# Two more row groups of batch 1 in seven block products, an earlier weight sum and other planned lengths of attention

## The chip, the core and the metric

The kernel runs on one core of one Trainium2 chip. The metric is the device time of one execution in microseconds (us). A core has TensorE (PE; its weight loads are listed apart as PEld), VectorE (DVE), ScalarE (ACT), GpSimd (POOL) and SyncE (SP), which here only issues transfers. Each engine works through its own list of instructions in order; semaphores hold an instruction until what it needs is there.

## What is computed

Chunked attention with a few memory keys, then a Fourier mix, a normalisation and two matrices with a Relu between them:

```python
# attention: 4 batches, 8 heads, 768 rows, 64 per head; chunks of 32 rows,
# each sees 16 rows to its left, 8 to its right and 8 memory rows
scores = scale * np.matmul(q_c, k_full.transpose(0, 1, 3, 2))
a = softmax(scores)
out[:, :, c_start:c_end] = np.matmul(a, v_full)
...
# x: 4 x 768 x 512, the heads side by side
mixed = np.real(np.fft.fft(np.fft.fft(x, axis=1), axis=2))
u = x + mixed
un = (u - mean(u)) / np.sqrt(var(u) + 1e-06)
ch = np.maximum(un @ w_ch1, 0.0) @ w_ch2      # w_ch1: 512 x 2048, w_ch2: 2048 x 512
return u + ch
```

## The kernel before

**Tiles.** A batch's 768 rows are six tiles of 128. Attention takes a pair of heads at a time, n = 0 to 15, four pairs a batch: loads of q and k from POOL's queue and of v from SP's, turns of q and k (on TensorE for batches 0 to 2, as transfers from SP's queue for batch 3), two groups of scores (`e_scores`, line 461), exponentials on ACT, values (`e_values`, line 485) and a division on DVE. `fourier(b)` then folds the rows on DVE (`zy`, `pq`, `ff`, `hi`, `lo`), multiplies by tables of cosines and sines on TensorE (`e_rows` at line 557, `e_columns` at line 727) and adds the result to the rows. For batches 1 to 3 the mirrored rows take a way through memory: out by `e_rows_out` (POOL, line 591), turned by `e_rows_turn` (SP, line 595), back by `e_mirror` (POOL, line 600), added by `e_sum_back` (DVE, line 615).

**Normalisation.** `e_stats` leaves mean and variance of a tile (line 741). A batch is then treated in one of two ways. In the plain way `e_un` writes mean - u (line 748), the Relu takes it with scale -1, and 1 / sqrt(var), made for the whole batch by `e_rstd` on POOL (line 785), multiplies the sum at the very end in `e_res` (line 828). In the other way `e_scale` on POOL (line 764) makes 1 / sqrt(var) and the shift for two tiles at a time, and `e_un` writes the normalised rows (line 752). `e_flip` turns a tile by a transfer from SP's queue (line 776) into `unT`, which has five buffers. The tiles `rs` of `e_scale` and `rstd` of `e_rstd` share two buffers.

**The two matrices.** A batch has three groups (b, j) of 256 rows: tiles 0 and 3, 4 and 5, 1 and 2 (`SLOT`). The first matrix, `e_ch1` (line 803), is eight steps of eight matmuls with 256 columns, each followed by a Relu into `hT` (line 812), of which there is one buffer. The second matrix of a plain group, `e_ch2` (line 821), is 2 x 16 matmuls with 512 columns, and `e_res` adds each half to u. A group in the list `FAST` does it as seven block products. There hT of the group is a 2 x 2 of blocks (two halves of the 2048 inner values, two tiles of rows) and w_ch2 a 2 x 2 of blocks (the same two halves, two halves of 256 columns). `e_s` (line 858) makes sums and differences of the blocks of hT on DVE, `e_w2t` (line 845) four of the weights, once for the whole kernel. `e_prod` (line 870) is eight matmuls with 256 columns for each of seven products, in the order 1, 2, 5, 6, 3, 7, 4, into the banks x, v and w; `e_add` (line 875) adds a product, or a running sum of them, to a half of u. The first three weight sums go to a tile of their own, which takes the place of hT of (0, 1); the fourth overwrites one block of w_ch2, so it waits for the last plain group. Products wait for the first three sums, product 4 for the fourth as well.

**The order.** Nothing is left to chance at run time: `Plan` simulates the engines with a length for each task and writes out the instructions in the order in which its tasks start. Attention and the Fourier mix have ranks in the order in which they are added; the two matrices have ranks from `MLPS` on, so they fill what the others leave of TensorE; Relus, residuals, sums on hT and adds have the lowest ranks and go first on their engines. The weight sums have ranks from `MLPS` on. After 45 us a task on TensorE that is no filler may be placed up to `SLACK` = 0.7 us before its inputs are due. `shortest(24, 1.5)` draws 24 disturbances of the ranks of all tasks after batch 0's attention and Fourier mix and keeps the order whose planned end is first. PSUM banks (`acc` and `mlp`, two each) are taken and given back in the plan; ph, the products' banks and one of the two value tiles take whichever of the two kinds came free first. The buffers of rs, rstd and the statistics are not in the plan.

`attention(n)`, lines 971 to 1045, adds the tasks of a pair with their lengths; `columns_of(b, t_rest)` those from the columns to the turned tiles; `layer1`, `layer2` and `weight_sums` those of the two matrices.

Of the kernel before, what the change touches and what calls it, by code (L numbers as in the profile page):

```python
# [205 lines left out]
def kernel(  # L206
# [12 lines left out]
    B, H, S, D = q.shape  # L219
# [44 lines left out]
    qs = [spool.tile([P, 2, RB * D], BF16, name=f"qs{i}") for i in range(NS)]  # L264
# [6 lines left out]
    kTb = [spool.tile([P, NT, P], BF16, name=f"kTb{i}") for i in range(NKT)]  # L271

    TURNED = 3
    FAST = [(b, j) for b in range(2, B) for j in range(3)]
    EVEN = {b for b, j in FAST}
    cp_q = "p h j d -> p h (j d)"
    HP = H // 2
    seq = [(b, pr) for b in range(B) for pr in (0, 2, 1, 3)]
# [138 lines left out]
    def e_turn_q(n):  # L417
        tr_of[n] = trq = aps.tile([P, S], BF16, tag="tr", bufs=1, name="trq")
        turn(trq, qs[n % NS][0:QP], ident_b[0:QP, 0:QP])
# [317 lines left out]
    def e_stats(b, kt):  # L737
# [3 lines left out]
        nc.vector.bn_stats(st6, xs[b][:, kt, :])  # L741
        nc.vector.bn_aggr(mu_of[b][:, kt, :], st6)

    def e_un(b, kt):
        un_of[b, kt] = un = fpool.tile([P, DM], FP16, tag="un", bufs=6, name="un")

        if b not in EVEN:
            nc.scalar.activation(un, xs[b][:, kt, :], AFT.Identity, bias=mu_of[b][:, kt, 0:1],
                                 scale=-1.0)
            return  # L750
        rs = rs_of[b][:, kt]
        nc.scalar.activation(un, xs[b][:, kt, :], AFT.Identity, bias=rs[:, 1:2], scale=rs[:, 0:1])  # L752
# [22 lines left out]
    def e_flip(b, kt):  # L775
        nc.sync.dma_start_transpose(unT(b, kt), un_of.pop((b, kt)))
# [29 lines left out]
    def e_relu(b, j, i):  # L806
        if i == 0:
            shape = [P, 2, HH, 2 * P]
            hT_of[b, j] = (wpool.tile(shape, FP16, tag="w2t", bufs=1, name="hT") if (b, j) == (0, 1) else
                           fpool.tile(shape, FP16, tag="hT", bufs=1, name="hT"))  # L810
        ph = ph_of.pop((b, j, i))
        nc.scalar.activation(hT_of[b, j][:, :, i, :], ph, AFT.Relu, bias=0.0,  # L812
                             scale=1.0 if b in EVEN else -1.0)
        let_go(ph)

    def e_ch2(b, j, r, part):
# [7 lines left out]
    def e_res(b, j, r):  # L824
        u, pc = xs[b][:, slot(b, 2 * j + r), :], pc_of.pop((b, j, r))
        st = slot(b, 2 * j + r)
        if b not in EVEN:
            nc.vector.scalar_tensor_tensor(u, pc, rstd_of[b][:, st:st + 1], u, ALU.mult, ALU.add)  # L828
        else:
            nc.vector.tensor_tensor(u, pc, u, ALU.add)  # L830
        let_go(pc)
# [139 lines left out]
    def attention(n):  # L971
# [20 lines left out]
        if b >= TURNED:  # L992
            eq = add("SP", 1.2, lambda: e_flip_q(n), [lq], take=("qT",), give=("qs",),
                     late=5.0, loose=True, behind=t_flip[0])
            t_flip[0] = tk = add("SP", 1.2, lambda: e_flip_k(n), [lk, t_uz, t_used.get(("kU", n % NKU))], take=("kU",),
                                 give=("ks",), late=5.0, loose=True, behind=eq)
            ek = add("DVE", 0.6, lambda: e_kT(n), [tk, mk], give=("kU",), lag=4.0)
            t_used["kU", n % NKU] = ek
        else:
            tq = add("PE", 0.46, lambda: e_turn_q(n), [lq, t_idb], take=("tr",), give=("qs",))  # L1000
            dve = ("DVE", nc.vector.tensor_copy) if n < HP else ("ACT", None)
            eq = add("ACT", 0.80, lambda: e_qT(n), [tq], take=("qT",), give=("tr",),
                     rank=SINES - 0.5 if n == 0 else None)
            ktag = "acc" if first else "tr"
            tk = add("PE", 0.48, lambda: e_turn_k(n), [lk, t_idb, t_kz if n == 0 else t_kzs],
                     take=(ktag,), give=("ks",))
            ek = add(dve[0], 1.25 if dve[1] else 1.04, lambda: e_kT(n, dve[1]), [tk, mk],
                     give=(ktag,))
        t_used[0, at], t_used[1, at] = (eq, tk) if b >= TURNED else (tq, tk)
        xs_ = []  # L1010
        for g in range(2):
            s_ = add("PE", 0.30, lambda g=g: e_scores(n, g), [eq, ek], take=("sc",),
                     give=("qT", "kTb") if g == 1 else (),
                     behind=t_sc.get((n, 0)))
            t_used["kTb", n % NKT] = s_
            t_sc[n, g] = s_
            t_exp[n, g] = x_ = add("ACT", 1.05, lambda g=g: e_exp(n, g),
                     [s_, t_masks, t_after.get(n)], take=("e1",), give=("sc",))
            xs_.append(x_)
            if not first and g == 0:  # L1020
                continue
            tag = "mlp" if first and g == 1 else "xa"
            if not first:
                vp = dict(of=("mlp", "acc"))
                pick_of["v", n] = vp
                v_ = add("PE", 1.5, lambda: [e_values(n, i) for i in range(2)],
                         xs_ + [lv, t_low[n % NV]], take=("xa",), pick=vp, give=("e1", "e1", "va"))
                t_used["va", n % NV] = t_used["v", n] = v_
                for i in range(2):
                    t_norm[n, i] = add("DVE", 0.78, lambda i=i: e_norm(n, i),  # L1030
                                       [v_, t_norm[n - n % HP, 0] if (n % HP, i) != (0, 0) else None],
                                       take=("xsb",) if i == 0 and n % HP == 0 else (),
                                       give=(("xa",), (vp,))[i])
                continue
            v_ = add("PE", 0.85, lambda g=g: e_values(n, g), [x_, lv, t_low[n % NV]], take=(tag,),
                     rank=len(plan.tasks) + (50 if (n, g) == (2, 1) else 25) if first else None,
                     give=("e1", "va") if g == 1 else ("e1",),
                     behind=t_used.get(("v", n)))
            t_used["va", n % NV] = t_used["v", n] = v_
            take = ("xsb",) if g == 0 and n % HP == 0 else ()  # L1040
            t_norm[n, g] = add("DVE", 0.78, lambda g=g: e_norm(n, g),
                               [v_, t_norm[n - n % HP, 0] if (n % HP, g) != (0, 0) else None],
                               take=take,
                               give=(tag,))
# [166 lines left out]
    def columns_of(b, t_rest):  # L1211
# [29 lines left out]
                           take=("acc",), rank=len(plan.tasks) + (15 if kt == 3 else 0),  # L1241
                           give=give)

        t_sum = {}
        columns(kts[0])
        for i, kt in enumerate(kts):
            if i + 1 < NST and not (b > 0 and kts[i + 1] == 3):
                columns(kts[i + 1])
            if b == 0 or kt < 3:
                su = add("DVE", 0.7, lambda kt=kt: e_sum(b, kt), [cols[kt]],  # L1250
                         give=("acc",) if b == 0 else ())
                t_sum[kt] = su
                if b > 0 and kt == 0:
                    columns(3)
            else:
                su = add("DVE", 0.8, lambda kt=kt: e_sum_back(b, kt - 3),
                         [cols.get(kt), t_sum[kt - 3], t_xr[b]],
                         give=("acc", "dn") if kt == 5 else ("acc",))
            sa = add("DVE", 0.9, lambda kt=kt: e_stats(b, kt), [su, sa])
            if b in EVEN:  # L1260
                if i % 2:
                    t0, t1 = kts[i - 1], kt
                    sc_ = add("POOL", 1.7, lambda t0=t0, t1=t1: e_scale(b, t0, t1 - t0), [sa])
                    for t in (t0, t1):
                        un = add("ACT", 0.78, lambda t=t: e_un(b, t), [sc_], take=("un",))
                        t_un[t] = add("SP", 1.2, lambda t=t: e_flip(b, t), [un],
                                      behind=t_un.get(kts[kts.index(t) - 1]) if t else None,
                                      take=room(t), give=("un",), late=2.5, loose=True)
                continue
            un = add("ACT", 0.78, lambda kt=kt: e_un(b, kt), [sa], take=("un",))  # L1270
            if b > 0:
                t_un[kt] = add("SP", 1.2, lambda kt=kt: e_flip(b, kt), [un],
                               behind=t_un.get(kts[i - 1]) if i else None,
                               take=room(kt), give=("un",), late=2.5, loose=True)
                continue
            tp = add("PE", 0.26, lambda kt=kt: e_turn_u(b, kt), [un, t_idh], take=("mlp",),
                     give=("un",))
            t_un[kt] = add("DVE", 0.43, lambda kt=kt: e_unT(b, kt), [tp, t_un.get(kt - 1)],
                           take=room(kt), give=("mlp",))
        return t_un, add("POOL", 2.05, lambda: e_rstd(b), [sa]) if b not in EVEN else None  # L1280

    mlp_prev, t_sums, side_end = [None], [], []
    PLAIN = [(b, j) for b in range(B) for j in range(3) if (b, j) not in FAST]
# [163 lines left out]
```

## Time and profile before

| | |
|---|---|
| median of 3 runs | 280.53 us (280.51 to 280.87) |
| the profiled execution | 280.87 us, its span 279.2 us |
| granted TensorE clock | 1.00 throughout |
| (1, 0), second matrix, TensorE | 137.27 to 151.79 us, among other work |
| (1, 1), second matrix | 161.39 to 168.30 us |
| (1, 2), second matrix | 177.71 to 185.49 us, among scores |
| (2, 0), (2, 1), (2, 2) and batch 3 in seven products | from 194.04 us on |
| the four weight sums, DVE | 106.03, 109.70, 126.88 and 186.26 us, 1.22 us each |
| last matmul starts | 275.7 us |

The span is cut into the work of five engines. A line of a timeline gives the start, the time from the first start to the last end of a run of like instructions, the engine, the source line, what is written and read, and how many there are; where the engine stood idle before it, the end of the line says for how long and for whom. TensorE's matmuls are pipelined, so the durations of neighbours overlap; the time that a run of them takes is the distance from its first start to the next run's.

### The profile page before, as it was taken

Reading aid. Unit: us, or ns where it says so; the run is one execution under the profiler, and the core shown is the slowest. Engines: PE = TensorE matmul, PEld = TensorE weight load, DVE = VectorE, ACT = ScalarE, POOL = GpSimd, SP = SyncE. Lnnn points to the kernel's source line nnn. Section 1 sums busy time; section 2 is a strip of 40 time slices with the busy share of each in tenths; the row PEclk is TensorE's granted clock in tenths of the full one; section 3 lists DMA queues with packets and bytes.
Section 4 is the critical chain, followed back from the end, with each engine's and each line's share of the span. In section 5 each row is a group of like instructions: output and inputs, shape, how many; then the busy total and the mean of one; then the engine's idle time right before and its main releaser. Section 6 shows DMA issues by size and latency. Waiting matters only on the chain.

```text
span 279.2 us, 7959 instructions
## 1 busy us (share of the span) xinstructions
PE 264.8 (95%) x3318; PEld 208.3 (75%) x3318; DVE 192.6 (69%) x424; ACT 154.7 (55%) x262; POOL 63.5 (23%) x127
## 2 busy tenths in 40 slices
PE   0599999999999999999999999999999999999995
PEld 0387797888765668758767857668889888888884
DVE  7968999941238999999937851259987975353444
ACT  6888647788777527636653556328164191605150
POOL 8852572330201096050211130001100130000000
PEclk9999999999999999999999999999999999999999
DMA  5998999999998999979992586824842057303152
GB/s 95 209 177 159 184 191 203 196 198 194 197 198 216 122 226 165 139 193 156 268 162 78 109 137 178 152 78 137 98 183 40 0 96 149 97 38 77 54 100 76
DMA packets 116116, 39.98 MB, mean 143 GB/s; under 512 B 104560, under 2 KB 111472, under 8 KB 116080
## 3 DMA queue, kind: packets, MB, share of 16 engines
q1 hardware_dynamic: 93888, 23.54, 45.6%
q0 software_dynamic: 21472, 15.21, 33.3%
q10 hardware_dynamic: 720, 0.72, 0.7%
q8 instruction: 26, 0.43, 0.7%
q14 instruction: 10, 0.08, 0.1%
HBM read 37.36 MB, written 13.37 MB: 182 GB/s over the span
## 4 chain that ended last, share of the span: by engine, by line
PE 82%; DVE 6%; POOL 5%; DMA 2%; ACT 2%; issue 2%; POOLq 0%; DVEq 0%
PE ph L803 26%; PE pc L821 15%; PE pc L870 11%; PE ps L557 6%; PE pm L727 5%; PE xa L485 4%; PE xo L485 4%; PE ps L716 3%; PE sc L461 3%; DMA qs<-in_q_dram 2%; PE trq L405 2%; PE trk L405 1%; PE idle L930 1%; ACT un L752 1%; PE pm L608 1%
## 5 line engine op out<-in xcount | busy, mean ns | idle before, releaser
L803 PE MATMUL ph<-unT,w_sb 128*128 128x256 f16 x768 | 90.0, 273 | 0.2 <-ACT hT L812 0.2
L812 ACT ACTIVATE hT<-ph 128x512 f16<-128x512 f32 x96 | 56.8, 597 | 47.3 <-PE ph L803 27.5
L803 PEld LDWEIGHTS <-w_sb 128*128 128x128 f16 x768 | 73.6, 98 | 10.8 <-issue 0.8
L821 PE MATMUL pc<-w_sb,hT 128*128 128x512 f16 x192 | 44.7, 380 | 0.0
L469 ACT ACTIVATE e<-sc,mbias 128x384 f32<-128x384 f32 x64 | 33.6, 580 | 17.7 <-PE sc L461 17.7
L821 PEld LDWEIGHTS <-hT 128*128 128x128 f16 x192 | 17.6, 98 | 19.2 <-issue 0.2
L870 PEld LDWEIGHTS <-hT 128*128 128x128 f16 x240 | 23.3, 98 | 3.9 <-issue 1.0
L875 DVE TENSOR_TENSOR xsb<-pc,xsb 128x256 f32<-128x256 f32 x43 | 17.8, 420 | 9.6 <-PE pc L870 8.4
L870 PE MATMUL pc<-w_sb,hT 128*128 128x256 f16 x192 | 24.1, 273 | 0.2 <-DVE xsb L875 0.2
L828 DVE SCALAR_TENSOR_TENSOR xsb<-pc,rstd,xsb 128x512 f32<-128x512 f32 x12 | 9.0, 749 | 18.8 <-PE pc L821 18.8
L569 ACT CAST up<-ps 128x386 f16<-128x386 f32 x16 | 9.7, 603 | 21.4 <-PE ps L557 20.4
L741 DVE BATCH_NORM_STATS2 st<-xsb 128x6 f32<-128x512 f32 x24 | 16.5, 687 | 0.5
L858 DVE TENSOR_TENSOR S<-hT 128x768 f16<-128x768 f16 (+1 forms) x12 | 5.1, 424 | 16.4 <-ACT hT L812 15.8
L485 PEld LDWEIGHTS xa<-va,e 128*64 128x64 f32 x384 | 13.1, 143 | 3.6 <-issue 2.9
L485 PE MATMUL xa<-va,e 128*64 128x65 f32 x384 | 15.4, 232 | 0.0
L752 ACT ACTIVATE un<-xsb,rs 128x512 f16<-128x512 f32 x12 | 9.5, 807 | 10.1 <-POOL rs L767 10.1
L485 PE MATMUL xo<-va,e 128*64 128x65 f32 x384 | 14.5, 227 | 0.0
L461 PEld LDWEIGHTS <-kTb 64*128 64x128 bf16 x384 | 7.7, 97 | 8.0 <-issue 5.3
L485 PEld LDWEIGHTS xo<-va,e 128*64 128x64 f32 x384 | 13.0, 142 | 0.4 <-ACT ff L651 0.3
L542 ACT CAST hi<-ff 128x768 f16<-128x768 f32 x12 | 9.9, 830 | 4.9 <-DVE ff L534 4.7
L461 PE MATMUL sc<-qT,kTb 64*128 64x64 bf16 x384 | 11.6, 196 | 0.9 <-POOL va L345 0.9
L870 PE MATMUL pc<-w_t,S 128*128 128x256 f16 x96 | 11.6, 272 | 0.4 <-DVE xsb L875 0.4
(168 smaller groups left out, 442.3 us busy)
## 6 DMA issues: line engine op xcount, KB each, us to landing
va<-in_v_dram SPq DMA_DIRECT2D x32, 220.0 KB
w_sb<-in_moe_w_ch_dram POOLq DMA_DIRECT2D x8, 512.0 KB, 14.5
out_dram<-xsb SPq DMA_DIRECT2D x12, 256.0 KB
qs<-in_q_dram POOLq DMA_DIRECT2D x12, 192.0 KB, 6.7
ks<-in_k_dram POOLq DMA_DIRECT2D x12, 192.0 KB, 6.7
x_rows<-xsb POOLq DMA_DIRECT2D x3, 768.0 KB, 4.6
xr<-x_back POOLq DMA_DIRECT2D x3, 768.0 KB, 6.0
out_rows<-xsb SPq DMA_DIRECT2D x9, 256.0 KB
```

Source lines behind the costliest of these rows:

```text
L461: nc.tensor.matmul(sc[:, hh, t6, :], kT[r0:r0 + 64, t, :], qT[r0:r0 + 64, ts(t, 64)], start=True, stop=True, tile_position=(r0, 0))
L469: nc.scalar.activation(e1[:, :, :, ts(half, 32)], sc[:, :, 0:6, ts(half, 32)], AFT.Exp, bias=mbias[:, half:half + 1], scale=1.0 / math.sqr ...
L485: nc.tensor.matmul(xa[64 * half:64 * half + 64, st, hh, 0:65], e1[:, hh, t6, :], v1[:, hh, 6 * g + t6, 0:65], start=True, stop=True)
L557: nc.tensor.matmul(out_[:, sp, :], part[:, ab, sp * 3 + st, c0:c1], tab[:, sp, st, :], start=(st == 0 and i == 0), stop=(st == 2 and i == 1))
L727: nc.tensor.matmul(pm[:, par, :], lhs, rhs[:, par, :], start=(im == 0), stop=(im == 3))
L741: nc.vector.bn_stats(st6, xs[b][:, kt, :])
L752: nc.scalar.activation(un, xs[b][:, kt, :], AFT.Identity, bias=rs[:, 1:2], scale=rs[:, 0:1])
L803: nc.tensor.matmul(ph[:, k, :], w1_sb[:, dt, ts(HH * k + i, P)], unT_of[b, j][:, dt, :], start=(dt == 0), stop=(dt == NDT - 1))
L812: nc.scalar.activation(hT_of[b, j][:, :, i, :], ph, AFT.Relu, bias=0.0, scale=1.0 if b in EVEN else -1.0)
L821: nc.tensor.matmul(pc_of[b, j, r], hT_of[b, j][:, k, i, ts(r, P)], w2_sb[:, HH * k + i, :], start=(i + k == 0), stop=(i + k == HH))
L870: nc.tensor.matmul(pc_of[key], a[:, i, :], w[:, i, :], start=(i == 0 and new), stop=(i == HH - 1), skip_group_check=not new)
L875: nc.vector.tensor_tensor(u, pc, u, ALU.add)
```

## The change

`FAST` gains (1, 1) and (1, 2), so batch 1 has a plain group, (1, 0), and two in seven products. What was asked of a batch (`EVEN`) is asked of a group or a tile (`even(b, kt)`), and batch 1 is `MIXED`: tiles 0 and 3 go the plain way, tiles 1 and 4 and then 2 and 5 through `e_scale`, with tile 1 held back until tile 4's statistics are there; the order of the turns becomes 0, 3, 1, 4, 2, 5, each behind the one before. `e_rstd` of batch 1 stays, for the plain group. The last plain group is now (1, 0), so the four weight sums are added to the plan behind it. Outside batch 0 the planned lengths on TensorE become 0.56 for a turn (0.46 and 0.48 before), 0.37 for a group of scores (0.30) and 1.64 for the values of a pair (1.5).

```diff
-    FAST = [(b, j) for b in range(2, B) for j in range(3)]
-    EVEN = {b for b, j in FAST}
+    FAST = [(1, 1), (1, 2)] + [(b, j) for b in range(2, B) for j in range(3)]
+    MIXED = 1
...
+    def even(b, kt):
+        return (b, SLOT.index(kt) // 2) in FAST
+
     def e_un(b, kt):
...
-        if b not in EVEN:
+        if not even(b, kt):
             nc.scalar.activation(un, xs[b][:, kt, :], AFT.Identity, bias=mu_of[b][:, kt, 0:1],
                                  scale=-1.0)
             return
...
         nc.scalar.activation(hT_of[b, j][:, :, i, :], ph, AFT.Relu, bias=0.0,
-                             scale=1.0 if b in EVEN else -1.0)
+                             scale=1.0 if (b, j) in FAST else -1.0)
...
-        if b not in EVEN:
+        if (b, j) not in FAST:
             nc.vector.scalar_tensor_tensor(u, pc, rstd_of[b][:, st:st + 1], u, ALU.mult, ALU.add)
...
-            tq = add("PE", 0.46, lambda: e_turn_q(n), [lq, t_idb], take=("tr",), give=("qs",))
+            tq = add("PE", 0.46 if first else 0.56, lambda: e_turn_q(n), [lq, t_idb], take=("tr",), give=("qs",))
...
-            tk = add("PE", 0.48, lambda: e_turn_k(n), [lk, t_idb, t_kz if n == 0 else t_kzs],
+            tk = add("PE", 0.48 if first else 0.56, lambda: e_turn_k(n), [lk, t_idb, t_kz if n == 0 else t_kzs],
...
-            s_ = add("PE", 0.30, lambda g=g: e_scores(n, g), [eq, ek], take=("sc",),
+            s_ = add("PE", 0.30 if first else 0.37, lambda g=g: e_scores(n, g), [eq, ek], take=("sc",),
...
-                v_ = add("PE", 1.5, lambda: [e_values(n, i) for i in range(2)],
+                v_ = add("PE", 1.64, lambda: [e_values(n, i) for i in range(2)],
...
-            if b in EVEN:
+            if b > MIXED or b == MIXED and even(b, kt):
+                if kt == 1 and b == MIXED:
+                    continue
                 if i % 2:
-                    t0, t1 = kts[i - 1], kt
+                    t0, t1 = kts[i - 1] if b > MIXED or kt == 5 else 1, kt
                     sc_ = add("POOL", 1.7, lambda t0=t0, t1=t1: e_scale(b, t0, t1 - t0), [sa])
                     for t in (t0, t1):
                         un = add("ACT", 0.78, lambda t=t: e_un(b, t), [sc_], take=("un",))
-                        t_un[t] = add("SP", 1.2, lambda t=t: e_flip(b, t), [un],
-                                      behind=t_un.get(kts[kts.index(t) - 1]) if t else None,
+                        t_un[t] = t_one = add("SP", 1.2, lambda t=t: e_flip(b, t), [un],
+                                      behind=t_one,
                                       take=room(t), give=("un",), late=2.5, loose=True)
                 continue
...
-                t_un[kt] = add("SP", 1.2, lambda kt=kt: e_flip(b, kt), [un],
-                               behind=t_un.get(kts[i - 1]) if i else None,
+                t_un[kt] = t_one = add("SP", 1.2, lambda kt=kt: e_flip(b, kt), [un],
+                               behind=t_one,
                                take=room(kt), give=("un",), late=2.5, loose=True)
...
-        return t_un, add("POOL", 2.05, lambda: e_rstd(b), [sa]) if b not in EVEN else None
+        return t_un, add("POOL", 2.05, lambda: e_rstd(b), [sa]) if b <= MIXED else None
```

More of the change, by code (lines that the diff above doesn't have):

```diff
@@ L1242, in columns @@
                            give=give)
-        t_sum = {}
+        t_sum, t_one = {}, None
         columns(kts[0])
```

## The prediction

> **What bounds the kernel now.** I read the page's busy table and its chain of waits first, then TensorE's timeline from 20 us to the end, then those of DVE, POOL and SP around the pieces that the change touches.
>
> ```profile
> span 279.2 us, 7959 instructions
> PE 264.8 (95%) x3318; PEld 208.3 (75%) x3318; DVE 192.6 (69%) x424; ACT 154.7 (55%) x262; POOL 63.5 (23%) x127
> PE 82%; DVE 6%; POOL 5%; DMA 2%; ACT 2%; issue 2%; POOLq 0%; DVEq 0%
> ```
>
> TensorE is busy for 264.8 of 279.2 us, and nearly all of its 14.4 idle us lie in the first 20 us (10.09 busy there) and in the last 3, where the result leaves. The list of TensorE's waits has two after 23 us: 0.6 us for the adds of line 875 and 0.2 us for a Relu (stops shorter than the 0.16 us by which durations run past the next start don't show there). So in the middle the time is the sum of what TensorE is given, and I price blocks of matmuls from start to start, since the durations overlap. The timeline has one plain second layer, of rows (1, 1), with nothing between its matmuls, and one in seven products, of (3, 1):
>
> ```profile
> 161.39 7.07 PE L821 MATMUL pc<-w_sb,hT 128*128 128x512 f16 x32
> 168.30 1.04 PE L803 MATMUL ph<-unT,w_sb 128*128 128x256 f16 x8
> ...
> 256.27 1.91 PE L870 MATMUL pc<-w_sb,hT 128*128 128x256 f16 x16
> 258.02 1.91 PE L870 MATMUL pc<-w_t,S 128*128 128x256 f16 x16
> 259.94 1.03 PE L870 MATMUL pc<-w_sb,hT 128*128 128x256 f16 x8
> 260.81 1.04 PE L870 MATMUL pc<-w_t,hT 128*128 128x256 f16 x8
> 261.68 1.04 PE L803 MATMUL ph<-unT,w_sb 128*128 128x256 f16 x8
> 262.56 1.04 PE L870 MATMUL pc<-w_sb,hT 128*128 128x256 f16 x8
> 263.43 6.28 PE L803 MATMUL ph<-unT,w_sb 128*128 128x256 f16 x56
> ```
>
> The columns are start, length, line, operands and count. The plain block takes 168.30 - 161.39 = 6.91 us, 216 ns a matmul. The seven products take 263.43 - 256.27 = 7.16 us less 0.88 for the foreign group at 261.68: 6.28. Of this 56 x 109.2 ns = 6.12 is streaming and 0.17 a stop ahead of 259.94, where product 3 waits for DVE (1.92 for a group that streams in 1.75). Where other work lies between the products, as in (2, 1) at 212.97 to 223.43, there is no stop.
>
> **The change, part by part.**
>
> *Seven products for (1, 1) and (1, 2).* 64 matmuls of 512 columns leave, 112 of 256 come. Streaming: 2 x (6.91 - 6.12) = 1.59 us off a TensorE that has no gap there. Stops given back, from both sides: none, as in (2, 1), or 0.58 a block, as in (2, 0):
>
> ```profile
> 195.78 1.04 PE L870 MATMUL pc<-w_t,S 128*128 128x256 f16 x8
> 197.23 1.03 PE L870 MATMUL pc<-w_t,S 128*128 128x256 f16 x8 [0.41 <-DVE xsb L875]
> ```
>
> (eight matmuls stream in 0.87, the next group starts 1.45 after.) I take 0.17 for each: for (1, 1) because nothing lay between its matmuls before, for (1, 2) as the nearer of the two, though scores came between its matmuls at 180.40 and 182.51. Net -1.25, bounds -1.59 and -0.43.
>
> The Trainium skill has a rule that speaks against this. Its page "TensorE: Matmul & The Clock Gate", section "Back-to-back issue gap", gives 131 ns for each of a stream of 512-column matmuls with their weight loads, and 81 ns at 128 columns. By it, with about 98 ns between them for 256 columns as an estimate, a plain block is 4.2 us and a fast one 5.5, and the change would lose 2.6 us. The trace disagrees at 216 and 109 ns; the same section's figure for the isolated gap, columns over 2.4 GHz plus 2.5 ns, gives 215.8 and 109.2 and is what the rows show, at a granted clock of 1.00.
>
> *DVE.* A fast block has seven adds (line 875, 0.42) and seven sums on hT (line 858: three of 0.555, three of 0.288, one of 0.68), 6.15 us, for two residuals of 0.75 (line 828): +4.65 a block, +9.3 in all. DVE was busy for 10.1 of 16.7 us in 151.8 to 168.5 and for 3.7 of 17.5 us in 168.5 to 186, so both blocks fit; the stops above are what is left of them on the path. The statistics of batch 2 fill DVE up to 162.1, just where the sums on hT of (1, 1) become ready (its Relus end at 162.5); if these queue behind, the block pays up to the 0.58.
>
> *The weight sums.* Three already run at 106.03, 109.70 and 126.88, ahead of (1, 1) at 161; their order stays behind everything else on DVE. The fourth, which waits for the last plain block, goes from behind (1, 2) to behind (1, 0), which ends at 151.8:
>
> ```profile
> 185.60 0.75 DVE L828 SCALAR_TENSOR_TENSOR xsb<-pc,rstd,xsb 128x512 f32<-128x512 f32 x1 [3.09 <-PE pc L821]
> 186.26 1.21 DVE L845 TENSOR_TENSOR w_sb<-w_sb,w_t 128x2048 f16<-128x2048 f16 x1
> 187.40 0.19 DVE L495 RECIPROCAL zs<-xa 128x6 f32<-128x6 f32 x1
> ```
>
> DVE has no gap from here to 208, and the stop of 0.58 in (2, 0) is its backlog. Residual and sum (1.80 us) go, two or three adds of 0.42 come, so about 0.7 us of that backlog is gone. Worth 0 to 0.58; I take -0.2. At 152 the sum is 10 us ahead of its reader, product 4 of (1, 1).
>
> *Batch 1's normalisation.* Tiles 1, 4, 2, 5 are scaled by rstd before they are turned: two more e_scale, 1.63 us each on POOL by 149.97 to 151.60, four activations at 0.807 for 0.724 (+0.33 on ACT). POOL stood idle there, 8.97 us ahead of 120.31. The turn of tile 1 waits for tile 4's statistics, those of 2 and 5 for a scale: SP's last turn of the batch, 118.58 to 123.78 now, gets one to two us later, and with it, queued behind on SP, the turns of k and q (123.88, 126.25) and, past those, the stores at 127.70. Their first reader is kTb's copy at 137.71; the turned tiles are read at 151.8. Cost 0; without this cover, the two us.
>
> rstd and rs share two buffers, and with rs of batch 1 between them rstd of batch 1 falls on that of batch 0, last read by the residual at 128.02. POOL may stand there from 120.3 to 128.8. Behind it: x_rows of batch 2 (121.97, 4.6 to landing) and the load of q at 122.81 (turned at 161.65). The rows' turn on SP (133.30) would start some 2.5 us later, the mirror (142.99, 6.0 to landing) land at 151.5; line 615 reads it at 155.82. Cost 0, by 4 us of cover; beyond it batch 2's tiles are 18 us early for (2, 0) at 187.04.
>
> *The plan's lengths.* No instruction changes, but the order on every engine from batch 1 on is chosen anew, by the search over 24 draws. Real pieces: scores 0.28 us, turns 0.47, values 1.55, and about 0.1 lost at the change of shape ahead of each (66.73 + 16 x 0.109 = 68.48, the turn starts at 68.58). So the new lengths are nearer to the trace; they put 4.8 us more into the plan (8 x 0.46 and 4 x 0.28). TensorE's gain is bounded by the stops that there are: 0.23 at 118.4, 0.32 at 233.39, 0.58 at 197.23, three of 0.17: 1.6 us, of which the last 40 us cannot move much. A loss has no such bound (below). I take +0.2.
>
> Sum: -1.25 - 0.2 + 0.2 = **-1.25 us**. The profiled execution took 280.87 us, 1.67 around its span of 279.2; its span would be 277.95 and its time 279.6. The median of the three runs, 280.53, lies 0.34 under it, so the forecast is **279.3 us**.
>
> **Rivals.** The measurement tells a change of 0.2%, 0.56 us, from none.
>
> *A: DVE's queue takes the gain (280.1).* Both blocks pay 0.58 and (2, 0) keeps its own: -0.43. For it: the statistics up to 162.1, and that adds stand in order behind operations of 0.95 us. Against: DVE's 12 idle us in 168.5 to 186.
>
> *B: the new order makes TensorE stop (281.6, slower).* The planner lets a piece of attention or of the transform go to TensorE up to SLACK = 0.7 us before its input is due. So far the plan gave these 52 attention pieces about 0.09 us less than they take, so real inputs were early; the new lengths take this cover away between 43 and 190 us. Price: four stops of 0.58 are 2.3 us, 280.53 - 1.25 + 2.3. It decides from 1.25 + 0.56 = 1.8 us of new stops, three of that size. Against: the transform's and the two layers' lengths were already true (rows 1.02 planned, 1.01 in the trace; 0.875 and 0.874), and from 187 to 223 they show one stop.
>
> *C: the end is not TensorE's (280.5).* If batch 3's transform set the end, the gain would go ahead of (3, 0). (3, 0) needs tiles 0 and 3, turned from 223.69 and from 228.05 on; the later ends near 229.4, for matmuls at 235.14: 5.7 us of cover against 1.25.
>
> *D: the new order also clears stops (278.5).* -1.59, -0.45 at (2, 0) and 118.4.
>
> *E: wide matmuls stream cheaper than the narrow ones by column,* so that 56 narrow ones lose: 283.1 if a wide one took 131 and a narrow one 98 ns. The rows at 216 and 109 speak against it wherever they are read. That page of the Trainium skill, above, would have it so.
>
> **How the numbers follow.** Forecast 0.61, D 0.07: faster 0.68. A 0.11 and C 0.02: within 0.2%, 0.13. B 0.17 and E 0.02: slower 0.19. The forecast's own range is 278.7 to 279.9, from the bounds of blocks, backlog and order. For 8 in 10 I go down to 278.2, for D and a little more, and up through A into the lower half of B, 281.3.
>
> **What would show it.** Line 821 with 128 matmuls, line 870 with 448, of the same 216 and 109 ns start to start; TensorE's busy time some 1.5 us less. Line 828 x8, 875 x57, 752 x16, 748 x8, 764 x8. The fourth weight sum near 152. Stops ahead of product 3 of (1, 1) and (1, 2) of at most 0.2, and a smaller one in (2, 0). (3, 0) starting 1 to 1.5 us earlier than 236.88, and the tail behind it as now. Wrong if TensorE's waits between 43 and 190 us add up to over 1 us (B), if either block lasts over 6.6 us (A), or if the blocks gain and (3, 0) waits for its tiles (C).

## The result and the profile after

The changed kernel takes 282.55 us (median of 5 runs, 281.63 to 283.38); the kernel before took 280.63 us beside it (5 runs, 280.51 to 280.91). The ratio is 1.0062, 95% interval 1.0047 to 1.0077: slower by 1.3 to 2.2 us, where 279.3 us was forecast. The profiled execution took 282.55 us, too. Its page begins, and its chain of waits is shared out, like this:

```profile
span 280.6 us, 8090 instructions
PE 264.2 (94%) x3365; PEld 213.0 (76%) x3365; DVE 201.1 (72%) x448; ACT 153.9 (55%) x262; POOL 66.6 (24%) x135
PE 63%; DVE 20%; DMA 8%; POOL 3%; ACT 2%; issue 2%; SPq 0%; POOLq 0%; DVEq 0%
```

TensorE has hardly less busy time (264.2 us, overlaps counted), and its share of the chain that sets the end fell from 82 to 63%: DVE and transfers now hold a part of it. The list of TensorE's waits (line, who was waited for, us in total, times, longest) had 0.6 us for the adds and 0.2 for a Relu after 23 us; now it has

```profile
PE pc L873 <- ACT hT L815: 0.9, 1, 0.9
...
PE pc L873 <- DVE xsb L878: 0.8, 3, 0.4
PE pm L727 <- DVE xsb L617: 0.7, 1, 0.7
PE ph L806 <- DVE xsb L831: 0.3, 1, 0.3
```

(The file is three lines longer from line 744 on: 803 is now 806, 821 is 824, 870 is 873.) TensorE's timeline has their places:

```profile
154.97 1.03 PE L806 MATMUL ph<-unT,w_sb 128*128 128x256 f16 x8 [0.33 <-DVE xsb L831]
156.72 0.39 PE L727 MATMUL pm<-cosD,up 128*128 128x256 f16 x2 [0.72 <-DVE xsb L617]
...
164.89 1.66 PE L873 MATMUL pc<-w_sb,hT 128*128 128x256 f16 x13
167.46 0.50 PE L873 MATMUL pc<-w_sb,hT 128*128 128x256 f16 x3 [0.90 <-ACT hT L815]
...
185.97 1.03 PE L873 MATMUL pc<-w_sb,hT 128*128 128x256 f16 x8 [0.43 <-DVE xsb L878]
187.17 1.03 PE L873 MATMUL pc<-w_t,hT 128*128 128x256 f16 x8 [0.17 <-DVE xsb L878]
```

The chain of waits in this stretch (start, us, what) runs past the second stop of this list and ends in the third:

```profile
141.48 0.59 SPq L595
...
142.12 6.08 DMA x_back<-x_rows
...
148.76 7.06 DMA xr<-x_back
...
155.91 0.69 DVE xsb L615
...
162.39 1.12 POOL rs L767
...
164.65 0.24 POOL rs L770
164.90 0.03 issue
164.92 0.02 ACT un L755
164.94 0.70 issue
165.64 0.58 ACT hT L815
166.22 0.70 ACT un L755
166.92 0.49 ACT hT L815
167.46 1.38 PE pc L873 x11
```

The rows of batch 2 leave for their mirror at 141.48 (133.30 before) and are back at 155.82. `e_sum_back` on DVE, line 615, waits for them, and the columns on TensorE for the bank that it frees. The statistics, the scale on POOL and `e_un` on ACT follow late, and the Relu that product 2 of (1, 1) needs stands in ACT's queue behind an `e_un` that waited for that scale. Whether the late rows make this third stop too, e3 tells below.

To add up such stops I take the distance from each matmul's start to the next, less the median for its shape. From 43 us on, in the profiled execution, this gives for before and after: streaming 219.1 and 217.6 us; stops of over 0.16 us 1.8 and 5.3; smaller losses, mostly where the shape changes, about 0.5 us less after. So the streaming gained 1.5 us, the smaller losses 0.5, the stops took 3.5, and the last product starts 1.45 us later (276.40 for 274.95). In the table below, *middle* is the distance from the first start of line 727 to the start of the last product's eight matmuls: 43.64 to 276.40 here, 232.8 us, and 231.3 before. It leaves out the head, which differs between the profiled executions. *Stops* are those of over 0.16 us.

| kernel | median, us (runs) | ratio to before, 95% interval | middle | stops |
|---|---|---|---|---|
| before | 280.63 | | 231.3 | 1.8 |
| after | 282.55 (5) | 1.0062, 1.0047 to 1.0077 | 232.8 | 5.3 |
| e1 lengths alone | 280.88 (12) | 1.0005, 0.9993 to 1.0017 | 231.1 | 1.6 |
| e12 lengths alone, draw 1 | 281.53 (12) | 1.0020, 1.0004 to 1.0036 | 231.9 | 2.9 |
| e2 products alone | 279.38 (6) | 0.9958, 0.9945 to 0.9972 | 230.1 | 2.4 |
| e5 products alone, draw 4 | 279.69 (7) | 0.9959, 0.9944 to 0.9974 | 230.0 | 2.4 |
| e6 products alone, draw 13 | 279.89 (11) | 0.9978, 0.9967 to 0.9990 | 230.7 | 2.5 |
| e4 after, draw 15 | 282.71 (5) | 1.0075, 1.0063 to 1.0088 | 233.3 | 5.5 |
| e7 after, draw 9 | 281.35 (11) | 1.0028, 1.0017 to 1.0039 | 232.2 | 4.0 |
| e8 after, draw 22 | 281.58 (12) | 1.0039, 1.0021 to 1.0056 | 231.3 | 3.8 |
| e3 after, rows first | 281.33 (12) | 1.0030, 1.0010 to 1.0050 | 232.0 | 4.5 |
| e10 after, slack 0 | 281.53 (12) | 1.0023, 1.0009 to 1.0036 | 232.2 | 4.8 |
| e11 after, inputs planned late | 283.25 (6) | 1.0085, 1.0060 to 1.0111 | 234.7 | 5.2 |
| e9 products, shorter lengths | 280.23 (12) | 0.9979, 0.9964 to 0.9993 | 230.3 | 3.2 |
| e13 products, values' length | 280.35 (10) | 0.9992, 0.9978 to 1.0005 | 230.8 | 2.9 |
| e14 products, scores' length | 280.64 (10) | 0.9998, 0.9986 to 1.0010 | 231.2 | 3.5 |
| e15 products, turns' lengths | 279.52 (4) | 0.9956, 0.9940 to 0.9972 | 230.1 | 2.6 |
| e16 products, lengths of batch 2 | 280.78 (10) | 1.0000, 0.9986 to 1.0015 | 230.9 | 3.4 |
| e17 products, lengths of batch 1 | 279.35 (10) | 0.9950, 0.9937 to 0.9963 | 229.7 | 1.7 |
| e18 products, lengths of batch 3 | 280.04 (10) | 0.9977, 0.9963 to 0.9992 | 230.4 | 2.4 |

Ratio and median are from repeated runs, middle and stops from one profiled execution each.

### The profile page after: what moved, and what is told of

It is laid out like the page before. It is cut to its first block, busy times and chain, and to the rows that moved or that the text cites. A ratio compares the mean times of both kernels' runs of the same rounds, so it can differ in the third digit from the quotient of the medians.

```text
span 280.6 us, 8090 instructions
## 1 busy us (share of the span) xinstructions
PE 264.2 (94%) x3365; PEld 213.0 (76%) x3365; DVE 201.1 (72%) x448; ACT 153.9 (55%) x262; POOL 66.6 (24%) x135
## 4 chain that ended last, share of the span: by engine, by line
PE 63%; DVE 20%; DMA 8%; POOL 3%; ACT 2%; issue 2%; SPq 0%; POOLq 0%; DVEq 0%
PE ph L806 26%; PE pc L873 14%; PE pc L824 6%; PE ps L557 4%; PE pm L727 3%; PE xa L485 3%; DMA qs<-in_q_dram 3%; DMA xr<-x_back 3%; DMA x_back<-x_rows 2%; DVE st L741 2%; PE sc L461 2%; PE xo L485 2%; DVE xsb L496 2%; DVE xsb L878 2%; PE trq L405 1%
## 5 line engine op out<-in xcount | busy, mean ns | idle before, releaser
L873 PEld LDWEIGHTS <-hT 128*128 128x128 f16 x320 | 31.0, 98 | 7.3 <-issue 1.8
L878 DVE TENSOR_TENSOR xsb<-pc,xsb 128x256 f32<-128x256 f32 x57 | 23.9, 422 | 15.3 <-PE pc L873 13.6
L873 PE MATMUL pc<-w_sb,hT 128*128 128x256 f16 x256 | 32.3, 273 | 1.6 <-ACT hT L815 0.9
L824 PE MATMUL pc<-w_sb,hT 128*128 128x512 f16 x128 | 30.0, 380 | 0.3 <-DVE up L574 0.3
L861 DVE TENSOR_TENSOR S<-hT 128x768 f16<-128x768 f16 (+1 forms) x16 | 6.8, 425 | 21.9 <-ACT hT L815 21.2
L755 ACT ACTIVATE un<-xsb,rs 128x512 f16<-128x512 f32 x16 | 12.5, 810 | 17.4 <-POOL rs L770 17.0
L824 PEld LDWEIGHTS <-hT 128*128 128x128 f16 x128 | 11.6, 98 | 13.1 <-issue 0.7
L873 PE MATMUL pc<-w_t,S 128*128 128x256 f16 x128 | 15.6, 273 | 0.0
L600 POOL DMA_DIRECT2D xr<-x_back x3 | 2.3, 783 | 48.0 <-DMA x_back<-x_rows 48.0
L873 PEld LDWEIGHTS <-S 128*128 128x128 f16 x128 | 12.4, 98 | 1.6
```

The costliest lines, as they stand in the source:

```text
L824: nc.tensor.matmul(pc_of[b, j, r], hT_of[b, j][:, k, i, ts(r, P)], w2_sb[:, HH * k + i, :], start=(i + k == 0), stop=(i + k == HH))
L873: nc.tensor.matmul(pc_of[key], a[:, i, :], w[:, i, :], start=(i == 0 and new), stop=(i == HH - 1), skip_group_check=not new)
```

## The experiments

### The two halves of the change, and the late rows

**e1: the new lengths alone, on the kernel before.**

```diff
-            tq = add("PE", 0.46, ...
+            tq = add("PE", 0.46 if first else 0.56, ...
-            tk = add("PE", 0.48, ...
+            tk = add("PE", 0.48 if first else 0.56, ...
-            s_ = add("PE", 0.30, ...
+            s_ = add("PE", 0.30 if first else 0.37, ...
-                v_ = add("PE", 1.5, ...
+                v_ = add("PE", 1.64, ...
```

> Work of the kernel before, with the new planned lengths of attention alone. Theory 1 (the new order is what costs: in it the mirrored rows of batch 2 come late and TensorE stops): 281.3 to 283. Theory 2 (the block products themselves cost, by DVE's queue, and the lengths do nothing): 280.2 to 281.0.

280.88 us, no change that can be told from none: in this order the new lengths do no harm by themselves, against theory 1.

**e2: the products alone:** the changed kernel with the old lengths, the diff above turned around.

> The two groups in seven products with the old planned lengths. Theory 1: the recorded sum without the lengths' 0.2, so about 279.2 (278.8 to 280.0), with stops in (1, 1) and (1, 2) of at most 0.6 each. Theory 2: 281.5 or more, with over 1.2 us of stops in the two blocks.

279.38 us, ratio 0.9958: 1.2 us faster than before, close to what was forecast for the whole change, and against theory 2. So most of the loss comes only when the products and the new lengths are together. Its page and TensorE's timeline:

```profile
span 277.4 us, 8086 instructions
```

```profile
157.11 0.38 PE L727 MATMUL pm<-cosD,up 128*128 128x256 f16 x2
...
160.61 1.91 PE L873 MATMUL pc<-w_sb,hT 128*128 128x256 f16 x16
162.35 1.93 PE L873 MATMUL pc<-w_t,S 128*128 128x256 f16 x16
164.71 1.03 PE L873 MATMUL pc<-w_sb,hT 128*128 128x256 f16 x8 [0.43 <-DVE xsb L878]
```

No wait stands at the columns (157.11), and the 16 matmuls of products 1 and 2 start without a break, though the mirror here lands at 155.1, only 0.7 us sooner than in the changed kernel: TensorE's order has the columns behind more of the first matrix. A stop of 0.6 us ahead of product 3 of (1, 1) (162.35 to 164.71 for 16 matmuls that stream in 1.75) and 0.26 further on remain; (1, 2) has none, and (2, 0) keeps its stop of 0.54.

**e3: the changed kernel, with one order altered: on SP the way of batch 2's rows (line 595) goes ahead of the turns of q and k of pair 14.** In the changed kernel SP's timeline has

```profile
137.90 1.22 SPq L410 DMA_TRANSPOSE qT<-qs  x1
139.28 2.09 SPq L414 DMA_TRANSPOSE kU<-ks  x1
141.48 0.59 SPq L595 DMA_DIRECT2D x_back<-x_rows  x1
```

```diff
+    t_turn = {}
...
+            t_turn[n] = (eq, tk)
...
-        for t in plan.shortest(24, 1.5):
+        placed = plan.shortest(24, 1.5)
+        for t in t_turn[14]:
+            placed = [p for p in placed if p is not t]
+        at = [p is t_x2[2] for p in placed].index(True)
+        for t in placed[:at + 1] + list(t_turn[14]) + placed[at + 1:]:
```

> The changed kernel with one thing moved, on SP alone: the turn of batch 2's rows goes ahead of the turns of q and k of pair 14. Theory 1: the two stops that the late rows make (0.89 and 1.08 in the changed kernel) go, 280.4 to 281.2, and the runs lie within 0.6 us of each other instead of 1.75. Theory 2: no change, 282 to 283.

281.33 us, just above what theory 1 forecast; the ratio falls from 1.0062 to 1.0030, about 0.9 us (the intervals just touch), the middle by 0.8. TensorE's timeline:

```profile
155.72 0.38 PE L727 MATMUL pm<-cosD,up 128*128 128x256 f16 x2
...
163.88 1.58 PE L873 MATMUL pc<-w_sb,hT 128*128 128x256 f16 x13
166.25 0.50 PE L873 MATMUL pc<-w_sb,hT 128*128 128x256 f16 x3 [0.79 <-ACT hT L815]
```

The wait at the columns is gone, as it had to be if the late rows made it; the stop for the Relu stays, at 0.95 us from start to start for 1.08. The mirror lands at 150.21 here, 5.6 us sooner, but line 615 on DVE starts only 1.2 us sooner, since DVE is at other work until then. DVE's timelines, of the changed kernel and of e3:

```profile
155.91 0.69 DVE L615 TENSOR_TENSOR xsb<-pm,xr 128x510 f32<-128x510 f32 x1 [1.00 <-DMA xr<-x_back]
```

```profile
154.05 0.74 DVE L831 SCALAR_TENSOR_TENSOR xsb<-pc,rstd,xsb 128x512 f32<-128x512 f32 x1
154.71 0.68 DVE L615 TENSOR_TENSOR xsb<-pm,xr 128x510 f32<-128x510 f32 x1
```

So the late rows make the stop at the columns and not the one for the Relu, which by e3's chain of waits hangs on DVE's own queue of sums and statistics ahead of the scale. The late rows are one part of the loss, about a third of what separates the changed kernel from e2.

### The luck of the draw, or the lengths

The lengths act only through the order that the search writes out, and any edit gives another. So I pinned other draws.

```diff
-        for i in list(range(tries)) + [None]:
+        for i in [15, None]:
```

**e4, e7, e8: the changed kernel with draw 15, 9 and 22. e5, e6: the products with the old lengths, draw 4 and 13. e12: the lengths alone, draw 1.**

> The changed kernel with the order of draw 15 in place of draw 8, the second best by the planner's own end. Theory 1: the order decides, so over 0.6 us from the changed kernel, to either side (279.5 to 284). Theory 2: the same work, so 282 to 283.

> Products with the old lengths (as e2, 279.38), order of draw 4, the second best by the planner's own end. Theory 3 (the spread between orders alone is as large as the loss, and the changed kernel drew a bad one): 279.4 to 282.5, over 0.6 from e2. Theory 4 (the new lengths lead to bad orders whenever the products are there): within 0.6 of e2, 278.8 to 280.0.

> Products with the old lengths, order of draw 13, the third best. Theory 3: 279.4 to 282.5, over 0.6 from e2 or from e5. Theory 4: 278.8 to 280.0.

> The changed kernel in the order of draw 9, the third best after draws 8 (the changed kernel) and 15 (e4, 282.71). Theory 3: 279.4 to 282.5, below 281.5 as likely as above. Theory 4: 282 to 283.5.

> The changed kernel in the order of draw 22, the fourth best. Theory 3: 279.4 to 282.5, below 281.5 as likely as above. Theory 4: 282 to 283.5.

> As e1 (280.88: the kernel before with the new lengths alone), in the order of draw 1, the second best. If the lengths are harmless without the products: 280.2 to 281.3. If e1 had a lucky order: 281.5 to 283.

With the products, three orders from the old lengths take 279.38 to 279.89 us, four from the new ones 281.35 to 282.71: the two sets don't meet, nor do they by the middle (230.0 to 230.7 us and 231.3 to 233.3). Between draws lie 0.5 us with the old lengths and 1.4 us with the new, between the sets 2 to 3 against e2. Both e7 and e8 lie below theory 4's 282 and within theory 3's range, but a spread of 1.4 us between orders is not as large as the loss, as theory 3 has it. The stops move from order to order (1.0 us at 155 in e4, 1.65 at 94 in e8, 0.85 at 217 in e7), and of those that the lengths add none stands in all four. The commonest kind, of 0.6 us ahead of product 3, comes in (1, 1) in e4 and e7, in (1, 2) in the changed kernel and e8, in (2, 0) in e4 and e7 and in (2, 1) in e4; but e2, e5 and e6 have it in (1, 1) as well, so one such stop belongs to the products and not to the lengths. Without the products the lengths cost 0 (e1) or 0.6 us (e12, at the edge of what was forecast if e1's order was a lucky one).

### Why truer lengths do harm: two ideas about cover

If the too short lengths served as cover, because TensorE then runs behind its plan and everything that feeds it is early, then a plan that lets TensorE wait for no input before it is due should restore it (e10), as should later inputs in the plan (e11), and still shorter lengths should do better (e9).

**e10: the changed kernel with no early placing.**

```diff
-    SLACK = 0.7
+    SLACK = 0.0
```

> The changed kernel with SLACK 0 in place of 0.7, so that no piece goes to TensorE ahead of its inputs in the plan. If the slack is the whole of it: 279 to 280. Theory 5: it concerns only attention and transform, while most stops stand before groups of the two matrices, so 281 to 282.5. Theory 6: 281.3 to 283.

281.53 us, 1.1 us better by the ratios than the changed kernel, and still slower than before. But e7 and e8, other draws that keep the slack, come as near (1.0028 and 1.0039 for 1.0023), so this one order doesn't show that the slack is a part of the loss.

**e11: the changed kernel; after 60 us each result of DVE, ACT and POOL is planned 0.23 us and each transfer 1.5 us later than so far.**

```diff
-                    t["done"] = at + (2.8 if q == "POOL" else 1.4) + t["late"]
+                    t["done"] = at + (2.8 if q == "POOL" else 1.4) + (1.5 if at > 60.0 else 0.0) + t["late"]
...
-                        t["done"] = now + cost + (t["late"] or self.LAG.get(e, 0.07))
+                        t["done"] = now + cost + (t["late"] or self.LAG.get(e, 0.07 if now < 60.0 else 0.3))
```

> The changed kernel, its true lengths kept, with the planner told after 60 us that each result of DVE, ACT and POOL is there 0.3 us after its end instead of 0.07, and each transfer 1.5 us later. Theory 5: cover comes back in another way, 279 to 280.5, with stops over 0.16 us of at most 3 us in sum. Theory 6: an order as bad as the others, 281.3 or more.

283.25 us, the slowest of all. Cover that is put into the plan in this way doesn't bring the time back.

**e9: the products with lengths as far below the old ones as the new are above.**

```diff
-            s_ = add("PE", 0.30, ...
+            s_ = add("PE", 0.30 if first else 0.23, ...
-                v_ = add("PE", 1.5, ...
+                v_ = add("PE", 1.36, ...
```

(turns 0.36 and 0.40.)

> Products with planned lengths of attention as far below the old ones as the new are above (turns 0.36 and 0.40, scores 0.23, values 1.36). Theory 5 (cover: a plan that gives attention less than it takes lets the other engines be early for TensorE, and the products need that): 278.8 to 280.0, with stops over 0.16 us of at most 2.5 us in sum. Theory 6 (any change of the lengths makes the order worse; the old ones were happily chosen): 280.5 to 283.

280.23 us, between the two forecasts: 0.6 us above e2 by the ratios, hardly more than e6, and better than every kernel with all the new lengths. In this one order shorter lengths do less harm than longer ones, and no good.

### Which length, and where

**e13, e14, e15: the products, with the values', the scores' or the turns' new length alone; e16, e17, e18: with all new lengths, for the pairs of batch 2, 1 or 3 alone.** In e13 and e16, for instance:

```diff
-                v_ = add("PE", 1.5, ...
+                v_ = add("PE", 1.64, ...
```

```diff
-            s_ = add("PE", 0.30, ...
+            s_ = add("PE", 0.37 if b == 2 else 0.30, ...
-                v_ = add("PE", 1.5, ...
+                v_ = add("PE", 1.64 if b == 2 else 1.5, ...
```

> The products, with the old lengths except that of the values (1.64 for 1.5; 12 pieces, 1.68 us more in the plan). Theory 4a (every longer length costs in proportion to what it adds to the plan, 4.8 us for a loss of 2 to 3): a third of it, 280.1 to 280.5 us, stops over 0.16 us of 3.0 to 3.6 us. Rival 4b (one of the three lengths carries the loss): 281.3 or more for that one and 279.3 to 279.9 for the other two. Rival 4c (any shift in the plan costs it, since the old lengths sit by luck at a good place): about 281 for all three.

> The products, with the old lengths except that of the scores (0.37 for 0.30; 24 pieces, 1.68 us more in the plan). Theory 4a: 280.1 to 280.5 us. Rival 4b: 281.3 or more if it is this length, 279.3 to 279.9 if it is another. Rival 4c: about 281.

> The products, with the old lengths except those of the turns of q and k of batches 1 and 2 (0.56 for 0.46 and 0.48; 16 pieces, 1.44 us more in the plan). Theory 4a: 280.0 to 280.4 us. Rival 4b: 281.3 or more if it is these, 279.3 to 279.9 if it is another. Rival 4c: about 281.

> The products, with all the new lengths, but for the four pairs of batch 2 alone (1.84 us more in the plan); batches 1 and 3 keep the old ones. If the loss starts with batch 2's attention ending late (its last values at 124.4 instead of 113.8 us, the mirrored rows at 155.8), as the stops between 154 and 168 us say, this one has most of it: 280.8 us or more, with the rows' mirror landing after 154 us. Theory 4a by the share of the plan: 280.2 to 280.6, whenever the mirror lands. Rival 4d (batch 3's attention, which ends 11 us earlier than before and pushes its transform's work on DVE into the block of (1, 2), is the cause): 279.3 to 279.9.

> The products, with all the new lengths for the four pairs of batch 1 alone (1.84 us more in the plan); batches 2 and 3 keep the old ones. One length alone gave 280.35 (values), 280.64 (scores) and 279.52 (turns), and all three for batch 2 alone 280.78. Theory 4a (the loss goes with what is added to the plan, wherever): 280.1 to 280.6 us. Rival 4e (the loss comes with batch 2's attention, which stands between the columns and the mirrored rows): 279.3 to 279.9 us, stops over 0.16 us of at most 2.9.

> The products, with the new lengths of scores and values for the four pairs of batch 3 alone (1.12 us more in the plan; its turns are not TensorE's). Theory 4a: 279.9 to 280.3 us. Rival 4e (batch 2's attention brings the loss): 279.3 to 279.9 us. Rival 4d (batch 3's attention, which ends 11 us earlier in the changed kernel, brings it): 280.8 us or more.

Against e2's ratio of 0.9958, the values' length costs 0.0034 (1.0 us), the scores' 0.0040 (1.1), the turns' nothing. Summed, the three cost 2.0 us, the lower end of what the four orders with all of them lose. None reached the 281.3 us of one length alone (4b), and any shift whatever (4c) has the turns and e17 against it; in proportion to what is added (4a) fits the values, nearly the scores (280.64 for at most 280.5), and fails for the turns, which add nearly as much, and for e17. By place, batch 1's lengths cost nothing (279.35), batch 2's 0.0042 (1.2 us), batch 3's 0.0019 (0.5), no more than e6, another draw. Batch 2's attention costs most here, 280.78 us where 280.8 or more was forecast. The way is another than was forecast: in e16 the mirror lands at 151.4, earlier than in e2, and the added stops (3.4 for 2.4 us) are small ones, at 96, at 118, in (2, 0) and behind. Where the late rows cost, as in the changed kernel, they are one outcome of a worse order among others. But each of these six is one order, and draws lie 0.5 to 1.4 us apart. By the middle, e13, e14 and e16 (230.8, 231.2, 230.9) are at most 0.5 us above e6 (230.7). So which length and which batch bring the loss is suggested and not shown.

## Why the prediction was wrong

**The step that failed is "The plan's lengths".** It argued that no instruction changes, that the new lengths are nearer to the trace, and took +0.2 us, with a gain bounded by 1.6 and a loss without bound. Nearer to the trace was no argument for a better order: with the products, the new lengths cost 2.0 to 3.3 us (ratios 1.0028 to 1.0075 against 0.9958), and with the old ones the time lies in the range of the forecast (279.4 to 279.9 us in three orders). The price that I left open was the largest term of the sum. A loss of this kind had been given to rival B, whose sign and place were right: TensorE's waits behind 150 us alone pass the 1 us that was to show it, and the time of 282.55 lies above its 281.6 and above the range. B's own mechanism, attention and transform placed up to the 0.7 us of `SLACK` ahead of their inputs, is not borne out. Of the stops behind 150 us only that of the columns stands at such a piece, and it waits for a bank that line 617 frees; `Plan` takes the slack off the times of inputs, not of banks, and the two matrices, where the others stand, get none. What e10 gained without the slack is no more than another draw gains with it.

**The step on the two blocks was right in kind, and in the size of the streaming; the stops were taken too small.** Streaming was to fall by 1.59 us and fell by 1.5; wide and narrow matmuls still take 216 and 109 ns, which ends rival E and the 131 ns of the Trainium skill's page "TensorE: Matmul & The Clock Gate", section "Back-to-back issue gap", on which it rests. For stops I took 0.17 a block and bounded them at 0.58. In e2 (1, 1) has 0.6 and 0.26, (1, 2) none: 0.85 for both against 0.34, so (1, 1) passes the bound by itself, and in e5 and e6 it has 1.08 and 1.25. The sign that was set for rival A is met by this, too: 6.12 us of streaming and 0.85 are more than 6.6. The stop is where the prediction put it, ahead of product 3, where the adds on DVE are waited for. In the changed kernel (1, 2) has 0.6 and 0.33 as well. That e2 came out at the forecast all the same is in part luck: its middle is 1.2 us shorter by 1.5 of streaming less 0.6 of added stops and about 0.3 of smaller losses that the prediction did not count on, and the order of e6 gains only 0.6 us.

**The backlog ahead of (2, 0), -0.2.** In e2 the stop there is 0.54, as before (0.57): nothing was gained by taking the weight sum away. In e5 and e6 0.29 and 0.36 stand in (2, 0), so the draw decides as much as the term was to bring. In the changed kernel the stop is gone, probably for another reason, which no run tests apart: batch 3's last values end at 175.7 instead of 187.1, its transform's work on DVE comes earlier, and (1, 2) has the stops in its place.

**The weight sum "near 152".** It runs at 162.22, since it stands behind batch 2's statistics in DVE's order; the products that read it start at 173.11, so it cost nothing either way.

**The normalisation, "cost 0, by 4 us of cover".** `e_rstd` did not wait for the residual at 128: POOL's timeline of the changed kernel has

```profile
120.83 0.25 POOL L788 TENSOR_SCALAR rstd<-mu_s 128x6 f32<-128x6 f32 x1 [2.70 <-ACT un L755]
```

so it came to a buffer that waits for `e_un` alone, and the 8.5 us were never there. The cover on the mirror was used up all the same: it lands at 155.1 in e2 and at 155.8 in the changed kernel, 149.8 before (6.8 us after its issue at 142.99, where the prediction reckoned with 6.0). The prediction looked at the transfer and not at the next thing that could change, namely when the new order of TensorE asks for its result. In e2 the columns start at 157.11 without a wait; in the changed kernel they are due 0.7 us before line 617 is done. A late landing alone costs nothing: in e17, as fast as e2, it is at 157.9.

**The tail.** From the first matrix of (3, 0) on all is as before, only later: 238.33 for 236.88.

**Two readings.** The stop at 118.4 was taken at its 0.23 us of idle time, beside others from start to start; measured like them it is 0.39, and the stops before are 1.8 us, not 1.6. DVE is idle for 13.8 us in 168.5 to 186 (17.5 less 3.7), not 12. Neither moves the forecast.

What stays open is why the truer lengths give worse orders. That cover on the inputs is the reason was argued and not shown: e10 can't be told from another draw, and e11 speaks against it in the form tried.

The kernel that beats both is the change without its new lengths, e2, at 279.38 us and 0.9958 of before (0.9945 to 0.9972); with the new lengths for batch 1 alone (e17) it is as fast, 279.35.

## What to carry to other kernels

Where a planner writes the order out, its lengths are tuned parameters: a change of them is a change of order, to be priced like an added mechanism of either sign, and tried apart from the change of work that it comes with. A cover that is counted from a transfer's landing to its old reader holds only as long as the reader keeps its place; after a new plan, ask first when each engine's new order will want it. To compare orders, pin several draws of each and take the distance between two fixed instructions, for one order says little.

## What the chip showed that I had not expected

The head of the kernel differs between the profiled executions by more than the changes in question. The first matmul of line 727 starts at 43.1 us in e2, at 44.3 in e18, whose 593 matmuls up to there are the same in the same order, and at 45.3 in e17, whose profiled execution took 280.89 us while the median of its runs is 279.35. With the middle alone e17 is the shortest of all, 229.7 us. Whether the head differs as much between executions of one kernel isn't shown, with one profiled execution of each.

The scatter of the runs differs, too: those of e2 lie within 0.7 us, those of the changed kernel within 1.8 and those of e3 within 2.9. It does not follow the stops: e4 has the most, 5.5 us, and its five runs lie within 0.5; e17 has 1.7, and its ten lie within 1.9.
